# Startup of a fused strided-sparse attention and ELU MLP kernel: fills ahead of loads, 80-row loads, and a new order of work

## The chip, the core and the metric

The kernel runs on one core of a Trainium2 chip. The metric is the device time of one execution in microseconds (us). The core has TensorE (PE; its weight loads are listed as PEld), VectorE (DVE), ScalarE (ACT), GpSimd (POOL) and SyncE (SP). Each takes its own instructions in program order and waits for the others by semaphores. Data moves by DMA, issued from SP, ACT or POOL.

## The reference

```python
# q, k, v: (8 batches, 8 heads, 576 positions, 64) fp32
scores = q @ k.T / 8                       # per batch and head
rel = pos[:, None] - pos[None, :]
mask_local   = (rel >= 0) & (rel < 32)                     # heads 0 to 3
mask_strided = (rel >= 0) & (pos_q % 32 == pos_k % 32)     # heads 4 to 7
attn = softmax(where(mask, scores, -1e9))
x = (attn @ v), heads side by side         # 4608 tokens x 512
h = x @ w_in                               # 512 -> 2048
out = elu(h) @ w_out                       # 2048 -> 512, fp32
```

## The kernel before

**Layout.** A position is written as p*8 + s, with s from 0 to 7 and p from 0 to 71. A load "by runs" (`load_runs`) brings, for each of four heads, 72 rows p of 8*64 elements, each row one run of 2 KB of fp32 in DRAM, and the POOL queue casts it to bf16 on the way. Strided attention (`s`) then only needs keys and queries with the same s modulo 4; local attention (`l`) works in windows of 96 queries and 128 keys. The tiles of a batch are called qs, ks, vs, ql, kl (by runs) and vl (six blocks of 96 rows for each head, in `vl_t`). Batch 1 is loaded into borrowed space: the end of `xT` and of `g[1]`.

**Attention.** Four pairs of heads for each batch: `0s0`, `0s1`, `0l0`, `0l1` for batch 0 and so on. For each pair q and k are transposed (batches 0 to 2 on PE, token `T`, copied out of PSUM by `c` on DVE or `C` on ACT; later ones by DMA, tokens `X` and `P`). For each half u of a pair: scores `S` (PE), exp `e` (ACT), mask `m` (DVE), product with v and row sums `O` (PE), log `n` and exp `r` of the sums (ACT, a reciprocal), and `x` (DVE), which writes the 512-wide activations `xT`.

**MLP.** Nine chunks of 512 tokens. For each of the 16 blocks of 128 hidden units: `L` (or its halves `a` and `b`) is the first product, `h` exp on ACT, `i` (DVE) or `j` (ACT) the clamp, `g` (DVE) the ELU into `g[0]` or `g[1]`. `Z.chunk.k.part` is the second product, `o` or `q` the copy out of PSUM (ACT or DVE), `t` the store. PSUM has eight banks; the last number of a token is the bank.

**Order.** Everything is written out by hand in the string `ORDER`: one token after another, and each engine takes its instructions in the order of the tokens. `D.x.b` is a load issued on POOL (`D.wi0` to `D.wi3` are the quarters of w_in, `D.wo0` to `D.wo3` those of w_out), `V` and `W` copies of v on DVE. `w` is a run of 42 matmuls on zeros at the start, and `K` casts the first pair's q (DVE) and k (ACT), which arrive as fp32 in `stage`, a piece of `g[0]`. `F` tokens are fills on DVE: `F.v0`, `F.v1` and `F.vs` write the constant columns of `vl_t[0]`, `vl_t[1]` and `vs_p`; `F.ks0` and the like write zeros into the half of the padded k tiles `kp` that no head uses; `F.ms` and `F.ml` make the masks, the latter from `mask_1`, which POOL makes.

**Before the tokens** there is a short prologue: the two stage loads (q on SP, k on ACT), the loads of qs and ks for heads 2 and 3 of the strided group, three memsets on DVE, then on POOL the loads of vs, ql, kl, vl, and after them `iota` and `mask_1`. In the tokens that follow, `F.v0` (L347) stands on DVE behind the load into the same tile `vl_t[0]` (L253), ahead of `F.ms`, both `K.q` and everything later on DVE:

```python
w.7.42 F.ks0 F.ks1 F.kl0 F.v1 F.vs F.v0 F.kl1 F.ms K.q.1 F.ml D.wi0.0 K.q.0 K.k.0 D.wi1.0 T.0s0.q.0
K.k.1 c.0s0.q T.0s0.k.7 D.wi2.0 T.0s1.q.6 c.0s0.k c.0s1.q D.wi3.0 S.0s0.1.01 S.0s0.0.23 e.0s0.1
```

**The end.** `copy_o` has a special case for the token `8.3` (`LAST`): the copy is cut in two halves, one on ACT and one on DVE, and its second store goes on ACT's queue. The order before ends with `Z.8.3`, `o.8.3`, `t.8.3`.

Of the kernel before, what the change touches and what calls it, by code (L numbers as in the profile page):

```python
# [15 lines left out]
S = 576  # L16
# [19 lines left out]
w.7.42 F.ks0 F.ks1 F.kl0 F.v1 F.vs F.v0 F.kl1 F.ms K.q.1 F.ml D.wi0.0 K.q.0 K.k.0 D.wi1.0 T.0s0.q.0  # L36
K.k.1 c.0s0.q T.0s0.k.7 D.wi2.0 T.0s1.q.6 c.0s0.k c.0s1.q D.wi3.0 S.0s0.1.01 S.0s0.0.23 e.0s0.1
T.0s1.k.7 e.0s0.0 m.0s0.1 c.0s1.k m.0s0.0 S.0s1.1.67 S.0s1.0.01 D.qs.1 e.0s1.1 O.0s0.1.23 e.0s1.0
D.ks.1 m.0s1.1 O.0s0.0.67 n.0s0.1 m.0s1.0 T.0l0.q.0 r.0s0.1 n.0s0.0 x.0s0.1 O.0s1.1.45 r.0s0.0
c.0l0.q D.vs.1 T.0l0.k.3 x.0s0.0 n.0s1.1 r.0s1.1 T.0l1.q.6 c.0l0.k T.0l1.k.7 x.0s1.1 C.0l1.q D.ql.1  # L40
V.0 S.0l0.1.01 S.0l0.0.56 c.0l1.k e.0l0.1 O.0s1.0.34 e.0l0.0 m.0l0.1 S.0l1.0.01 n.0s1.0 m.0l0.0
O.0l0.1.56 e.0l1.0 D.kl.1 r.0s1.0 m.0l1.0 S.0l1.1.01 n.0l0.1 x.0s1.0 e.0l1.1 O.0l0.0.34 r.0l0.1
m.0l1.1 O.0l1.0.01 x.0l0.1 n.0l0.0 O.0l1.1.56 r.0l0.0 D.vl.1 n.0l1.0 x.0l0.0 a.0.1.7 r.0l1.0 n.0l1.1
x.0l1.0 a.0.0.4 r.0l1.1 a.0.3.0 x.0l1.1 b.0.1 D.wo0.0 b.0.0 h.0.1 b.0.3 h.0.0 i.0.1 a.0.7.5 h.0.3
g.0.1 a.0.4.6 j.0.0 b.0.4 i.0.3 a.0.8.7 g.0.3 D.wo1.0 h.0.4 a.0.12.3 i.0.4 b.0.12 g.0.0 a.0.13.0
h.0.12 b.0.13 D.wo2.0 g.0.4 a.0.14.4 h.0.13 i.0.12 b.0.14 g.0.12 j.0.13 T.1s1.q.6 a.0.6.1 D.wo3.0
c.1s1.q h.0.14 b.0.8 g.0.13 a.0.9.6 h.0.8 i.0.14 b.0.7 D.fqs.0 g.0.14 j.0.8 a.0.2.0 b.0.9 h.0.7
g.0.8 a.0.5.4 h.0.9 i.0.7 a.0.10.3 D.fks.0 i.0.9 b.0.6 g.0.7 a.0.15.7 h.0.6 b.0.2 g.0.9 D.fql.0
b.0.15 h.0.2 i.0.6 b.0.10 g.0.6 h.0.15 b.0.5 h.0.10 i.0.2 T.1s0.k.6 T.1s0.q.5 i.0.15 D.qs.2 h.0.5
T.1l0.q.1 i.0.10 C.1s0.q a.0.11.2 g.0.15 b.0.11 C.1l0.q g.0.2 T.1s1.k.7 h.0.11 T.1l0.k.5 g.0.10  # L50
T.1l1.k.0 C.1s0.k i.0.5 T.1l1.q.1 D.ks.2 C.1l0.k i.0.11 Z.0.1.0.3 c.1l1.k C.1l1.q C.1s1.k g.0.11
S.1l1.1.56 S.1s0.0.01 e.1l1.1 g.0.5 Z.0.3.0.7 e.1s0.0 m.1l1.1 V.1 D.ql.2 S.1s1.0.45 S.1s1.1.01
e.1s1.0 Z.0.1.1.3 m.1s0.0 e.1s1.1 m.1s1.0 O.1l1.1.45 m.1s1.1 O.1s1.0.01 n.1l1.1 Z.0.3.1.7 r.1l1.1
n.1s1.0 D.kl.2 x.1l1.1 Z.0.1.2.3 r.1s1.0 x.1s1.0 O.1s1.1.45 Z.0.3.2.7 n.1s1.1 r.1s1.1 O.1s0.0.01
x.1s1.1 D.vs.2 Z.0.1.3.3 n.1s0.0 r.1s0.0 D.vl.2 S.1l0.1.45 o.0.1 x.1s0.0 Z.0.3.3.7 e.1l0.1 t.0.1
S.1l1.0.01 m.1l0.1 o.0.3 S.1s0.1.23 S.1l0.0.45 Z.0.0.0.6 e.1l1.0 t.0.3 e.1l0.0 m.1l1.0 O.1l0.1.01
Z.0.0.1.6 e.1s0.1 m.1l0.0 n.1l0.1 m.1s0.1 O.1l0.0.23 r.1l0.1 O.1s0.1.45 x.1l0.1 n.1l0.0 Z.0.0.2.6
n.1s0.1 r.1l0.0 r.1s0.1 Z.0.0.3.6 x.1l0.0 x.1s0.1 O.1l1.0.01 o.0.0 T.2s1.k.2 W.2 Z.0.2.0.3 n.1l1.0
t.0.0 r.1l1.0 c.2s1.k Z.0.2.1.3 x.1l1.0 V.2 L.1.2.0 L.1.1.1 h.1.2 i.1.2 L.1.0.2 h.1.1 g.1.2 L.1.8.4
i.1.1 h.1.0 g.1.1 j.1.0 L.1.5.0 h.1.8 g.1.0 L.1.4.1 h.1.5 i.1.8 i.1.5 L.1.6.2 h.1.4 g.1.8 Z.0.2.2.3  # L60
i.1.4 h.1.6 g.1.5 j.1.6 Z.0.2.3.3 g.1.4 g.1.6 T.2s1.q.0 o.0.2 L.1.7.1 c.2s1.q t.0.2 S.2s1.0.23 h.1.7
T.2s0.k.0 T.2s0.q.4 e.2s1.0 i.1.7 T.2l1.q.5 D.qs.3 c.2s0.q C.2s0.k L.1.3.6 g.1.7 C.2l1.q D.ks.3
m.2s1.0 S.2s0.0.34 h.1.3 T.2l1.k.5 D.vs.3 e.2s0.0 O.2s1.0.01 i.1.3 L.1.9.7 c.2l1.k n.2s1.0 m.2s0.0
L.1.11.2 r.2s1.0 g.1.3 h.1.9 O.2s0.0.34 x.2s1.0 h.1.11 T.2l0.q.6 T.2l0.k.5 n.2s0.0 i.1.9 D.ql.3
c.2l0.q L.1.15.0 r.2s0.0 g.1.9 L.1.10.1 i.1.11 h.1.15 x.2s0.0 C.2l0.k S.2s0.1.67 g.1.11 S.2s1.1.34
h.1.10 L.1.14.5 X.ks.3 i.1.15 e.2s0.1 i.1.10 D.kl.3 e.2s1.1 L.1.13.2 g.1.15 h.1.14 g.1.10 S.2l1.1.34
h.1.13 L.1.12.0 i.1.14 X.qs.3 m.2s0.1 j.1.13 g.1.14 O.2s0.1.67 e.2l1.1 Z.1.0.0.1 g.1.13 n.2s0.1
D.vl.3 m.2l1.1 P.s.3 h.1.12 S.2l0.0.23 S.2l1.0.45 m.2s1.1 Z.1.0.1.1 r.2s0.1 i.1.12 e.2l1.0 g.1.12
Z.1.0.2.1 e.2l0.0 x.2s0.1 O.2s1.1.45 m.2l0.0 O.2l1.1.23 n.2s1.1 S.2l0.1.67 W.3 Z.1.0.3.1 n.2l1.1
X.kl.3 m.2l1.0 r.2s1.1 Z.1.1.0.0 o.1.0 x.2s1.1 Z.1.1.1.0 r.2l1.1 D.qs.4 X.ql.3 e.2l0.1 x.2l1.1  # L70
O.2l0.0.45 D.ks.4 Z.1.1.2.0 n.2l0.0 m.2l0.1 D.vs.4 O.2l0.1.67 r.2l0.0 S.3s1.0.23 t.1.0 Z.1.2.0.1
n.2l0.1 x.2l0.0 e.3s1.0 Z.1.1.3.0 r.2l0.1 m.3s1.0 O.3s1.0.23 x.2l0.1 o.1.1 S.3s1.1.45 Z.1.2.1.1
n.3s1.0 t.1.1 e.3s1.1 O.2l1.0.67 Z.1.3.0.0 r.3s1.0 m.3s1.1 P.l.3 n.2l1.0 x.3s1.0 O.3s1.1.45
Z.1.3.1.0 X.ks.4 r.2l1.0 n.3s1.1 S.3s0.0.23 x.2l1.0 Z.1.3.2.0 e.3s0.0 r.3s1.1 L.2.8.6 m.3s0.0
x.3s1.1 L.2.4.7 h.2.8 D.ql.4 i.2.8 O.3s0.0.45 h.2.4 L.2.10.2 g.2.8 n.3s0.0 i.2.4 L.2.2.3 h.2.10
g.2.4 r.3s0.0 L.2.9.6 i.2.10 h.2.2 g.2.10 L.2.5.7 D.kl.4 h.2.9 i.2.2 x.3s0.0 j.2.9 L.2.1.2 g.2.2
h.2.5 S.3l1.0.45 g.2.9 h.2.1 L.2.11.3 e.3l1.0 i.2.5 i.2.1 L.2.6.6 h.2.11 D.vl.4 g.2.5 X.kl.4
S.3l0.1.45 g.2.1 h.2.6 L.2.7.7 i.2.11 e.3l0.1 i.2.6 L.2.14.2 m.3l1.0 h.2.7 m.3l0.1 O.3l1.0.45 g.2.6
h.2.14 Z.1.3.3.0 g.2.11 n.3l1.0 L.2.15.6 i.2.7 r.3l1.0 i.2.14 g.2.7 o.1.3 L.2.0.3 h.2.15 x.3l1.0
t.1.3 L.2.3.7 h.2.0 i.2.15 g.2.14 O.3l0.1.45 h.2.3 L.2.13.0 g.2.15 n.3l0.1 i.2.3 L.2.12.2 i.2.0  # L80
r.3l0.1 g.2.3 h.2.13 Z.1.2.2.1 x.3l0.1 h.2.12 S.3l1.1.67 i.2.13 S.3l0.0.45 e.3l1.1 g.2.0 Z.1.2.3.1
X.ql.4 e.3l0.0 g.2.13 S.3s0.1.67 o.1.2 Z.2.1.0.3 m.3l1.1 m.3l0.0 e.3s0.1 i.2.12 O.3l1.1.01 Z.2.2.0.4
X.qs.4 m.3s0.1 n.3l1.1 g.2.12 O.3s0.1.67 r.3l1.1 Z.2.2.1.4 W.4 n.3s0.1 x.3l1.1 P.l.4 Z.2.2.2.4
r.3s0.1 x.3s0.1 Z.2.2.3.4 P.s.4 O.3l0.0.67 o.2.2 Z.2.1.1.3 t.1.2 n.3l0.0 Z.2.1.2.3 r.3l0.0 t.2.2
Z.2.0.0.4 x.3l0.0 L.3.4.7 D.qs.5 L.3.5.6 D.ks.5 h.3.4 i.3.4 L.3.3.5 D.vs.5 h.3.5 g.3.4 D.ql.5
L.3.9.0 i.3.5 h.3.3 g.3.5 j.3.3 S.4s1.0.12 L.3.11.7 h.3.9 g.3.3 e.4s1.0 L.3.0.6 i.3.9 h.3.11 m.4s1.0
S.4s0.0.12 g.3.9 h.3.0 X.ks.5 L.3.10.5 i.3.11 e.4s0.0 i.3.0 L.3.8.0 h.3.10 m.4s0.0 g.3.0 j.3.10
D.kl.5 O.4s1.0.12 Z.2.0.1.4 g.3.11 n.4s1.0 g.3.10 h.3.8 O.4s0.0.67 Z.2.0.2.4 r.4s1.0 i.3.8 n.4s0.0
g.3.8 L.3.6.5 x.4s1.0 r.4s0.0 D.vl.5 Z.2.0.3.4 h.3.6 x.4s0.0 L.3.2.2 i.3.6 o.2.0 g.3.6 S.4s1.1.01
t.2.0 h.3.2 L.3.13.4 e.4s1.1 i.3.2 X.kl.5 L.3.12.5 g.3.2 h.3.13 m.4s1.1 j.3.13 L.3.1.0 h.3.12 g.3.13  # L90
O.4s1.1.12 h.3.1 S.4l0.1.67 i.3.12 Z.2.3.0.4 n.4s1.1 g.3.12 e.4l0.1 Z.2.1.3.3 i.3.1 r.4s1.1 m.4l0.1
S.4l0.0.67 g.3.1 o.2.1 L.3.7.5 x.4s1.1 e.4l0.0 t.2.1 L.3.14.3 h.3.7 m.4l0.0 i.3.7 O.4l0.1.67 h.3.14
O.4l0.0.12 g.3.7 L.3.15.0 n.4l0.0 i.3.14 n.4l0.1 Z.2.3.1.4 g.3.14 r.4l0.0 Z.2.3.2.4 r.4l0.1 x.4l0.0
h.3.15 Z.2.3.3.4 x.4l0.1 i.3.15 S.4l1.0.12 o.2.3 Z.3.1.0.7 g.3.15 e.4l1.0 t.2.3 Z.3.1.1.7 m.4l1.0
O.4l1.0.01 S.4s0.1.23 n.4l1.0 S.4l1.1.45 Z.3.1.2.7 X.qs.5 e.4s0.1 r.4l1.0 Z.3.1.3.7 m.4s0.1 e.4l1.1
x.4l1.0 O.4s0.1.23 o.3.1 Z.3.0.0.6 P.s.5 m.4l1.1 n.4s0.1 W.5 O.4l1.1.01 X.ql.5 r.4s0.1 Z.3.0.1.6
n.4l1.1 D.qs.6 x.4s0.1 Z.3.0.2.6 r.4l1.1 D.ks.6 Z.3.3.0.7 P.l.5 x.4l1.1 D.vs.6 Z.3.0.3.6 t.3.1
S.5s1.1.01 o.3.0 S.5s1.0.23 S.5s0.0.45 e.5s1.0 L.4.3.6 t.3.0 e.5s1.1 m.5s1.0 L.4.2.3 e.5s0.0 m.5s1.1
D.ql.6 h.4.3 X.ks.6 O.5s1.1.01 m.5s0.0 O.5s1.0.45 h.4.2 i.4.3 L.4.7.2 n.5s1.0 g.4.3 Z.3.3.1.7
n.5s1.1 i.4.2 r.5s1.0 g.4.2 L.4.0.6 r.5s1.1 x.5s1.0 D.kl.6 h.4.7 L.4.9.3 x.5s1.1 h.4.0 O.5s0.0.45  # L100
i.4.7 h.4.9 S.5l1.0.01 i.4.0 Z.3.3.2.7 n.5s0.0 g.4.7 e.5l1.0 g.4.0 L.4.1.2 r.5s0.0 i.4.9 D.vl.6
m.5l1.0 S.5s0.1.01 h.4.1 L.4.13.6 x.5s0.0 P.s.6 e.5s0.1 i.4.1 O.5l1.0.45 g.4.9 h.4.13 S.5l0.1.01
X.qs.6 Z.3.3.3.7 n.5l1.0 m.5s0.1 i.4.13 e.5l0.1 L.4.8.3 g.4.1 r.5l1.0 g.4.13 O.5s0.1.12 o.3.3 X.kl.6
L.4.15.0 x.5l1.0 h.4.8 n.5s0.1 L.4.11.7 W.6 h.4.15 i.4.8 D.qs.7 S.5l0.0.45 m.5l0.1 r.5s0.1 t.3.3
Z.4.0.0.6 g.4.8 D.ks.7 h.4.11 x.5s0.1 L.4.4.3 e.5l0.0 D.vs.7 i.4.15 j.4.11 O.5l0.1.45 m.5l0.0 h.4.4
L.4.10.1 g.4.15 n.5l0.1 i.4.4 L.4.6.0 g.4.11 h.4.10 r.5l0.1 i.4.10 L.4.12.2 g.4.4 h.4.6 L.4.14.7
# [47 lines left out]
def kernel(  # L154
# [150 lines left out]
    for nm in ("vs", "ql", "kl", "vl"):  # L305
        load(nm, 0)
# [406 lines left out]
```

## Time and profile before

| | before |
|---|---|
| median of 3 runs | 334.99 us (334.53 to 335.02) |
| the profiled execution's own time | 334.41 us |
| its span | 332.7 us, so 1.7 us lie around the span |
| PE busy | 307.3 us (92%) |
| DVE, ACT busy | 228.0 us (69%), 234.4 us (70%) |
| mean granted TensorE clock | 0.997 |
| DMA | 38.61 MB in 99319 packets; POOL's queue (q0) 18.66 MB, SP's (q1) 19.10 MB, ACT's (q10) 0.44 MB |

The profile gives one execution. Times count from the start of the span. In the timeline a row is start, duration, engine, line, operation, tiles and count; in brackets stands how long the engine was idle before it and what ended that. A busy PE is modelled and is not PE at its peak. DMA bytes are counted at the destination, so a casting load from fp32 counts half of what it reads.

### The profile page before, as it was taken

The page shows a single profiled execution, that of the slowest core. Times are in us where ns is not written, and L with a number is a line of the kernel's source. Part 1 is how long each engine was busy: PE and PEld are TensorE (multiplying, and loading weights), DVE is VectorE, ACT ScalarE, POOL GpSimd, SP SyncE. Part 2 cuts the span into 40 slices and gives each one's busy share as a digit, 9 for nine tenths or more (in the row PEclk, how much of TensorE's full clock was granted, in tenths as well). Part 3 has the DMA queues.
Part 4 walks back from the last instruction along what each step waited for, and adds up shares of the span by engine and source line. Part 5 has one row for each costly group of instructions (what it writes and reads, how often), then busy time and mean ns, then how long its engine had stood idle before and what let it go on. Part 6 is the DMA issues. An engine that isn't in the chain of part 4 may idle for free.

```text
span 332.7 us, 6428 instructions
## 1 busy us (share of the span) xinstructions
PE 307.3 (92%) x2410; PEld 158.8 (48%) x2410; DVE 228.0 (69%) x452; ACT 234.4 (70%) x408; POOL 75.6 (23%) x102
## 2 busy tenths in 40 slices
PE   5069999999989999999999999999999999999993
PEld 5056454446445445455554454455544444444441
DVE  5168796578966996788579979874589386447500
ACT  2038687868988897799799889689798675336320
POOL 8634230003920722630263205400000000000000
PEclk9999999999999999999999999999999999999998
DMA  7999997215999999999799989962400121111032
GB/s 148 187 206 188 206 196 69 65 32 92 155 183 140 184 134 180 169 94 141 155 208 129 175 152 157 110 163 61 131 14 0 35 62 32 33 34 53 10 92 69
DMA packets 99319, 38.61 MB, mean 116 GB/s; under 512 B 80568, under 2 KB 93112, under 8 KB 99288
## 3 DMA queue, kind: packets, MB, share of 16 engines
q0 software_dynamic: 65920, 18.66, 56.7%
q1 hardware_dynamic: 33128, 19.10, 27.1%
q10 hardware_dynamic: 240, 0.44, 0.4%
q8 instruction: 19, 0.31, 0.4%
q14 instruction: 12, 0.10, 0.1%
HBM read 37.84 MB, written 9.44 MB: 142 GB/s over the span
## 4 chain that ended last, share of the span: by engine, by line
PE 63%; DVE 12%; DMA 9%; ACT 8%; issue 4%; POOL 1%; SPq 0%; ACTq 0%; POOLq 0%; DVEq 0%
PE ps L636 30%; PE ps L602 25%; DVE g L630 4%; PE ps L440 3%; DVE he L619 3%; DMA kpl<-kTl 3%; DMA vl<-in_v_dram 3%; ACT e L447 3%; DVE xT L569 2%; DMA kTs<-ks 2%; ACT ln L538 2%; ACT he L610 2%; DMA kps<-kTs 2%; PE ps L510 1%; ACT rc L544 1%
## 5 line engine op out<-in xcount | busy, mean ns | idle before, releaser
L636 PE MATMUL ps<-w_out_sb,g 128*128 128x512 bf16 x576 | 136.6, 379 | 0.0
L602 PE MATMUL ps<-xT,w_in_sb 128*128 128x512 bf16 x576 | 135.1, 381 | 1.0 <-DVE g L630 0.8
L610 ACT ACTIVATE he<-ps 128x512 f32<-128x512 f32 x144 | 83.5, 595 | 31.8 <-PE ps L602 30.7
L602 PEld LDWEIGHTS <-w_in_sb 128*128 128x128 bf16 x576 | 54.5, 98 | 63.8 <-issue 4.7
L630 DVE TENSOR_TENSOR g<-he,ps 128x512 bf16<-128x512 bf16 x118 | 78.4, 681 | 6.4 <-PE ps L636 4.1
L636 PEld LDWEIGHTS <-g 128*128 128x128 bf16 x576 | 52.7, 98 | 56.3 <-DVE g L630 0.6
L619 DVE TENSOR_SCALAR he<-he 128x512 bf16<-128x512 f32 x118 | 50.9, 442 | 23.1 <-ACT he L610 22.4
L569 DVE TENSOR_TENSOR xT<-ps,rc 64x576 bf16<-64x576 f32 (+1 forms) x64 | 43.2, 679 | 23.2 <-ACT rc L544 22.3
L447 ACT ACTIVATE e<-ps 72x576 bf16<-72x576 f32 (+1 forms) x64 | 40.3, 647 | 18.0 <-PE ps L440 17.0
L538 ACT ACTIVATE ln<-ps 64x576 f32<-64x576 f32 (+1 forms) x64 | 36.9, 583 | 8.7 <-PE ps L510 6.2
L544 ACT ACTIVATE rc<-ln 64x576 f32<-64x576 f32 (+1 forms) x64 | 39.4, 620 | 1.5
L650 ACT COPY osb<-ps 128x512 f32<-128x512 f32 x32 | 18.7, 585 | 24.4 <-PE ps L636 24.3
L236 POOL DMA_DIRECT2D ql<-in_q_dram x20 | 16.5, 832 | 30.7 <-DMA qTl<-ql 27.9
L454 DVE TENSOR_TENSOR pm<-e,mask_s 72x576 bf16<-72x576 bf16 x32 | 14.4, 452 | 13.2 <-ACT e L447 12.8
L229 POOL DMA_DIRECT2D qs<-in_q_dram x7 | 5.5, 787 | 77.7 <-DMA qTs<-qs 45.3
L628 DVE SCALAR_TENSOR_TENSOR g<-he,ps 128x512 bf16<-128x512 bf16 x26 | 17.7, 680 | 1.1 <-ACT he L617 0.8
L460 DVE TENSOR_TENSOR pm<-e,mask_l 128x576 bf16<-128x576 bf16 x32 | 14.3, 453 | 4.5 <-ACT e L447 3.9
L617 ACT ACTIVATE he<-he 128x512 bf16<-128x512 f32 x26 | 16.4, 629 | 0.7
L243 POOL DMA_DIRECT2D kl<-in_k_dram x20 | 15.2, 776 | 5.8 <-DMA vs<-in_v_dram 2.8
L400 PE MATMUL ps<-identity,qs 72*128 72x72 bf16 x32 | 2.2, 226 | 12.8 <-DVE qs L387 12.8
L510 PEld LDWEIGHTS <-vl 128*128 128x128 bf16 x144 | 8.7, 96 | 6.4 <-issue 1.9
L503 PEld LDWEIGHTS <-vsp 72*128 72x128 bf16 x192 | 9.1, 98 | 5.4 <-issue 0.7
(91 smaller groups left out, 185.9 us busy)
## 6 DMA issues: line engine op xcount, KB each, us to landing
out_dram<-osb SPq DMA_DIRECT2D x31, 144.0 KB
vl<-in_v_dram POOLq DMA_DIRECT2D x8, 288.0 KB, 8.0
w_in_sb<-in_moe_w_in_dram POOLq DMA_DIRECT2D x4, 512.0 KB, 12.4
w_out_sb<-in_moe_w_out_dram POOLq DMA_DIRECT2D x4, 512.0 KB, 14.9
vs<-in_v_dram POOLq DMA_DIRECT2D x7, 288.0 KB, 7.5
qs<-in_q_dram POOLq DMA_DIRECT2D x6, 288.0 KB, 6.5
ks<-in_k_dram POOLq DMA_DIRECT2D x6, 288.0 KB, 8.6
kps<-kTs SPq DMA_DIRECT2D x10, 160.0 KB
```

The source lines that it names most:

```text
L236: nc.gpsimd.dma_start(out=t[0:RS, h % 2, :, h // 2, :], in_=q[b, h].rearrange("(p s) d -> p s d", s=NS))
L447: nc.scalar.activation(e[0:R], tiles.pop(("S", key, u))[0:R], ACT.Exp, scale=scale)
L538: nc.scalar.activation(t, s_ps, ACT.Ln)
L544: nc.scalar.activation(t, tiles.pop(("ln", key, u)), ACT.Exp, scale=-1.0)
L569: nc.vector.tensor_mul(dst, o_ps, rc)
L602: nc.tensor.matmul(tiles["h", ch, m], lhsT=w_in_sb[:, c, m * 128:(m + 1) * 128], rhs=xT[:, c, ch * CHUNK:(ch + 1) * CHUNK], start=(c == 2) ...
L610: nc.scalar.activation(e, tiles["h", i[0], i[1]], ACT.Exp)
L619: eng.tensor_scalar(e1, e, scalar1=1.0, scalar2=1.0, op0=ALU.min, op1=ALU.subtract)
L628: nc.vector.scalar_tensor_tensor(dst, e1, -1.0, h, op0=ALU.mult, op1=ALU.max)
L630: nc.vector.tensor_tensor(dst, e1, h, op=ALU.max)
L636: nc.tensor.matmul(ops, lhsT=g[ch % 2][:, m, kk * 128:(kk + 1) * 128], rhs=w_out_sb[:, m, :], start=(m == 0), stop=(m == MC - 1), skip_gro ...
L650: eng(o_sb, o_ps)
```

## The change

- **Fills first.** The fills of both `vl_t` tiles stand in the prologue on DVE, ahead of the loads into them; that of `vs_p` follows. The `F` tokens for them are gone, and so are those for `kp`.
- **Zeros on ScalarE.** The four zero halves of `kp` (64 x 664 or 64 x 592 32-bit words) are written by four ACT copies of a broadcast zero, right after ACT's table load; only the small edges stay on DVE.
- **iota** goes ahead of the loads on POOL.
- **80 rows.** `load_runs` and the stage loads bring 80 rows of a head instead of 72; rows 72 to 79 belong to the next head and fill what the DMA transposes read beyond the data. Where that would run past the tensor's end, 72 are kept. The three small loads that filled those rows before (`fill_rows`, tokens `D.fqs`, `D.fks`, `D.fql`) are gone.
- **One queue.** Both stage loads are issued on SP, q first.
- **F.ml** makes the mask by two copies with a broadcast instead of six.
- **A new order.** All tokens from the first to the last are arranged anew. Counts are the same but for: `c` 14 to 18 and `C` 10 to 6, `o` 33 to 32 and `q` 3 to 4. The order now ends with `Z.8.0.3 o.8.0 t.8.0`; token `8.3` is the last but one.

```diff
-    raw["vs"] = consts.tile([RS, HG * NS * D], BF16, tag="vs", name="vs")
+    raw["vs"] = consts.tile([RP, HG * NS * D], BF16, tag="vs", name="vs")
...
+    def runs(x, b, h, n):
+        rows = RP if (b * H + h + n - 1) * S + RP * NS <= B * H * S else RS
+        return rows, bass.AP(x.tensor, x.offset + (b * H + h) * S * D,
+                             [[NS * D, rows], [S * D, n], [1, NS * D]])
     def load_runs(nm, b, h0=0, n=HG):
...
-            out=t[0:RS].rearrange("p (h f) -> p h f", h=HG)[:, h0:h0 + n],
-            in_=x[b, hb:hb + n].rearrange("h (p s) d -> p h (s d)", s=NS))
+            out=rawof(nm, b)[0:rows].rearrange("p (h f) -> p h f", h=HG)[:, h0:h0 + n], in_=in_)
...
-    load_stage(nc.sync, 0, q)
-    load_stage(nc.scalar, 1, k)
+    load_stage(0, q)
+    load_stage(1, k)
...
+    nc.gpsimd.iota(dist, pattern=[[1, RS]], base=RS, channel_multiplier=-1)
+    for t in vl_t:
+        fill_ones(t, HG * LB)
+        nc.vector.memset(blocks(t, HG * LB)[0:PRE, 0, :], 0.0)
     for nm in ("vs", "ql", "kl", "vl"):
         load(nm, 0)
-    nc.gpsimd.iota(dist, pattern=[[1, RS]], base=RS, channel_multiplier=-1)
+    fill_ones(vs_p, HG * NS)
...
+    for (c, z), t in kp.items():
+        s_ = slice(2 * NS * RP, None) if c == "s" else slice(0, PRE)
+        nc.vector.memset(t[z * D:(z + 1) * D, s_], 0.0)
+        r = slice((1 - z) * D, (2 - z) * D)
+        w = t[r].bitcast(F32)
+        nc.scalar.copy(w, zero[r, 0:2].bitcast(F32).to_broadcast([D, w.shape[1]]))
...
             for u in range(2):
-                for i in range(3):
-                    nc.vector.tensor_copy(mask_l[:, u, :, i, :], mask_1)
+                nc.vector.tensor_copy(mask_l[:, u],
+                                      mask_1.unsqueeze(2).to_broadcast([128, NS, 3, LN]))
...
 ORDER
-w.7.42 F.ks0 F.ks1 F.kl0 F.v1 F.vs F.v0 F.kl1 F.ms K.q.1 F.ml D.wi0.0 K.q.0 K.k.0 D.wi1.0 T.0s0.q.0
-K.k.1 c.0s0.q T.0s0.k.7 D.wi2.0 T.0s1.q.6 c.0s0.k c.0s1.q D.wi3.0 S.0s0.1.01 S.0s0.0.23 e.0s0.1
+w.7.42 F.ms K.q.1 K.q.0 D.wi0.0 F.ml T.0s0.q.0 D.wi1.0 c.0s0.q K.k.0 K.k.1 D.wi2.0 T.0s1.q.0
+T.0s0.k.1 c.0s1.q D.wi3.0 T.0s1.k.2 c.0s0.k c.0s1.k S.0s0.0.01 S.0s0.1.67 e.0s0.0 S.0s1.1.45
...
-Z.8.2.3.1 Z.7.2.3.2 o.8.2 Z.8.1.0.1 t.8.2 o.7.2 Z.8.0.0.0 t.7.2 Z.8.0.1.0 Z.8.0.2.0 Z.8.0.3.0
-Z.8.1.1.1 o.8.0 Z.8.1.2.1 t.8.0 Z.8.1.3.1 Z.8.3.0.0 o.8.1 Z.8.3.1.0 t.8.1 Z.8.3.2.0 Z.8.3.3.0 o.8.3
-t.8.3
+t.7.1 o.7.2 L.8.5.1 t.7.2 h.8.0 i.8.0 L.8.7.7 h.8.5 g.8.0 L.8.2.6 i.8.5 h.8.7 g.8.5 L.8.3.0 h.8.2
+i.8.7 g.8.7 L.8.14.1 h.8.3 i.8.2 L.8.9.7 i.8.3 h.8.14 g.8.2 L.8.10.2 g.8.3 h.8.9 i.8.14 Z.8.2.0.0
+i.8.9 h.8.10 g.8.14 j.8.10 Z.8.2.1.0 g.8.9 g.8.10 Z.8.1.0.1 Z.8.2.2.0 Z.8.2.3.0 Z.8.1.1.1 o.8.2
+Z.8.1.2.1 t.8.2 Z.8.1.3.1 Z.8.3.0.0 o.8.1 Z.8.3.1.0 t.8.1 Z.8.3.2.0 Z.8.3.3.0 Z.8.0.0.1 o.8.3
+Z.8.0.1.1 t.8.3 Z.8.0.2.1 Z.8.0.3.1 o.8.0 t.8.0
```

## The prediction

> **What bounds the kernel now.** I read the page's slices first, then the list of waits, then the timeline of the first 50 us, and last the timeline of the end.
>
> ```profile
> PE   5069999999989999999999999999999999999993
> ...
> DMA  7999997215999999999799989962400121111032
> GB/s 148 187 206 188 206 196 69 65 32 92 155 183 140 184 134 180 169 94 141 155 208 129 175 152 157 110 163 61 131 14 0 35 62 32 33 34 53 10 92 69
> ```
>
> One slice is 8.3 us. From the fourth on PE is busy nine tenths; its hole is the second slice. DMA is full for six slices, to about 50 us.
>
> ```profile
> PE ps L400 <- DVE qs L387: 12.8, 1, 12.8
> ...
> DVE vl L347 <- DMA vl<-in_v_dram: 9.0, 1, 9.0
> ```
>
> PE waits once, 12.8 us, for DVE's cast of q, and DVE waited 9.0 us for a load before that. In order of time:
>
> ```profile
> 5.45 1.20 POOL L253 DMA_DIRECT2D vl<-in_v_dram  x1
> ...
> 6.36 1.14 ACT L387 CAST ks<-g 72x512 bf16<-72x512 f32 x2 [3.61 <-DMA g<-in_k_dram]
> ...
> 14.89 0.70 DVE L347 MEMSET vl<- 128x768 f32 x1 [8.95 <-DMA vl<-in_v_dram]
> ...
> 17.00 0.42 DVE L387 CAST qs<-g 72x512 bf16<-72x512 f32 x1
> ...
> 18.56 0.66 PE L400 MATMUL ps<-identity,qs 72*128 72x72 bf16 x8 [12.84 <-DVE qs L387]
> ...
> 20.72 1.19 ACT L447 ACTIVATE e<-ps 72x576 bf16<-72x576 f32 x2 [13.22 <-PE ps L440]
> ```
>
> The fill of vl waits for the load of the same tile, which lands near 14.8. k was cast at 6.36, and q's load was issued at the same time as k's: the first transposes wait for a fill that they don't need. The first exp starts at 20.72, the last `x` of batch 0 ends at 33.98 (33.52 + 0.46), and from 32.1 PE has the MLP to work on.
>
> **Part 1: the wait goes, and what is late next.** (a) DVE. The fills start after `mask_1`, at 1.22. From before's rows: each vl tile 0.70 + 0.09 + 0.07, twice 1.72; vs_p 0.91 + 0.09; ones, kTs, kTl 0.34; four small edges 0.08 + 0.08 + 0.07 + 0.07. That ends at 4.6. `F.ms` is 0.19 + 0.20 + 0.23 with gaps: 5.3. Its iota is ready at 3.6, since POOL does it after `identity` (3.36). The load of vl on POOL now waits for the fill, done at 2.1, and is issued only near 5.6: no cost. (b) q. No row shows its landing; k's row bounds it: not after 6.4 if q lands like k, and not before DVE is free at 5.3. I take 6.0, as q is first on its queue: casts 0.42 + 0.54, 7.0. (c) `F.ml` stands on DVE between the casts and `c.0s0.q`, and needs `mask_1` from POOL, which was done at 7.51 (7.20 + 0.31) and stays there, since iota has only changed places. So 7.55, and the six copies took 0.84 for the same elements that two now write, plus 0.10: 8.5. This is the next late thing. (d) `c.0s0.q` 0.46 (9.0), `T.0s1.q` 0.66 into the same bank (9.65), `c.0s1.q`, `c.0s0.k` 0.46 each (10.6), and from the end of the k copy (20.20) to the first exp (20.72) there were 0.52: first exp at 11.1, against 20.72, **9.6 us earlier**.
>
> Beside it lies k: ACT's table load ends at 2.75, then four zero copies. No row shows them; between 0.585 (128x512, L650) and 0.8 each, near the 0.65 of a 576-wide exp: 2.6 us, done at 5.4 (6.0 at most). k is issued 0.42 later (SP's issue of q takes 0.42), so 6.36 + 0.42 = 6.8, casts to 7.95: hidden under (c). Cover gone, it would cost nothing before 9.7, when `T.0s0.k` is due.
>
> (e) Batch 0's attention took 13.26 us from the first exp to the last `x`, with ACT nearly full: 8 exps of 0.65, 8 logs of 0.40, 8 exps of 0.44 and a copy of 0.64 are 12.6. The copy moves to DVE (`c.0l1.q`, 0.46), where it and `V.0` (0.55) now stand ahead of the mask `m.0l0.1` that PE and ACT wait for. I take no change, with -0.6 (the copy) and +1.0 (those two) as ends. The last `x` ends at 24.4. Sum of part 1: **-9.6** (-10.2 to -8.6).
>
> **Part 2: do the loads follow?** POOL's loads share eight semaphores, so each waits until the load eight before it has landed, and POOL's own waits tell the landings.
>
> ```profile
> 31.29 0.58 POOL L259 DMA_DIRECT2D qs<-in_q_dram  x1 [1.53 <-DMA g<-in_v_dram]
> ...
> 35.32 0.92 POOL L229 DMA_DIRECT2D qs<-in_q_dram  x1 [1.96 <-PE ps L602]
> ```
>
> Here the first wait is for vs of batch 1, and the last, though put down to PE, is for vl. Counted so through the timeline, w_in's quarters landed at 17.5, 20.2, 22.5 and 25.1, batch 1's q and k (strided) at 27.1 and 29.0, vs 31.3, ql 31.9, kl 32.8, vl 35.3, and w_out's at 37.8, 40.3, 42.8, 46.1. The queue runs at about 200 GB/s throughout, so an earlier PE brings nothing earlier. 80 rows add 32 KB to each load of 288 KB: for the nine such loads' worth of batches 0 and 1, 288 KB, 1.4 us. The three fill loads that go (96 KB, 0.5 us) came later. So batch 1 and w_out land up to 1.4 later.
>
> When are they due? After 24.4 PE does `a` and `b` halves at 2 x 0.216 (28 L602 matmuls took 6.04) and transposes at about 0.35. `T.1s1.q` comes after nine halves, 28.3, against 28.0 to 28.5; `T.1s0.k` near 30.1, against 30.4; `T.1l1.k` near 34, against 34.2. `V.1` stands on DVE behind 11 `g` (0.69), 9 `i` (0.43) and two copies (0.46): 12.4, with the first `h` near 25.4 about 37.4, against 36.7. `Z.0.0.0` comes at about 40, against 39.2, and its four parts follow at w_out's pace of 2.5 us. Everything is due within half a microsecond of its landing. I take **+1.0**, between 0 and 4 (if PE waits for each of w_out's parts, its last at 47.5 would stand against some 44 to 46).
>
> The rows again by the skill: 240 packets on q10 are 216 runs of data (144 for k, 72 for the last store) and 24 more, 12 for each of its two transfers. The Trainium skill, "DMA: Bandwidth & Descriptors", section "Why a DMA increments its semaphore by 16 and not by 1", says that a copy is spread over the largest number up to 16 that divides its slowest dimension, which makes 12 engines of 72 rows and 16 of 80. By that rule the stage loads alone would be some 0.2 us quicker, an estimate; the rows show a queue bounded by bytes, so the sum has nothing for it.
>
> A row also speaks on the clock: 8 transposes took 0.66 at 18.56 and 0.42 at 39.93, both at granted clock 1.00. The Trainium skill, "TensorE: Matmul & The Clock Gate", section "What's actually happening", has the array at half rate after about 3.4 us idle; by it the idle stretch before, 12.8 us, ends cold, while a gap of 2 us after the 42 zero matmuls need not. By an estimate from that rule the start would win up to 0.5 us more. The sum uses the slow row.
>
> **Part 3: the middle.** The work on PE from the first `L.1` on is the same, and PE's idle time between 32 and 300 us is 5.0 us by its windows (0.42, 1.58, 0.88, 0.69, 0.75, 0.67, 0). Four PSUM copies move from ACT to DVE (about 2 us of DVE, at 69%), `i` and `j` keep their counts. A new order can win back those 5.0 or add as much; nothing in the trace tells which, and I take **0**, between -3 and +3.
>
> **Part 4: the end.**
>
> ```profile
> 327.72 0.37 ACT L647 COPY osb<-ps 128x256 f32<-128x256 f32 x1 [2.87 <-PE ps L636]
> 328.12 0.42 DVE L648 COPY osb<-ps 128x256 f32<-128x256 f32 x1 [15.53 <-ACT osb L647]
> 328.57 0.32 SPq L663 DMA_DIRECT2D out_dram<-osb  x1
> 328.58 0.35 ACTq L663 DMA_DIRECT2D out_dram<-osb  x1
> ```
>
> Before this the last 80 matmuls run without a gap, 17.43 us from 310.21 to 327.64, and the last stores are issued 0.94 after PE's end, on two queues at once. In the new order eight `L.8` stand together and then `Z.8.2`. On DVE they cost seven `i` and eight `g`, 8.5 us from the first `h`, against 7 x 0.86 = 6.0 for PE: `Z.8.2.0` waits for `g.8.3` about 0.4, `Z.8.2.2` for `g.8.10` about 0.4. The last block is now 8.0: its tokens cross a row of the output twice, so one whole copy (0.59) and three stores on SP (0.36 each): the last is issued 0.08 + 0.59 + 0.05 + 0.72 = 1.44 after PE's end, 0.5 later. **+1.3**, between 0.3 and 2.
>
> **Sum.** -9.6 + 1.0 + 0 + 1.3 = -7.3. The profiled execution took 334.41 (332.7 + 1.7), so 327.1; the median of the runs lies 0.58 above it: **327.7 us**. About 0.2% (0.7 us) is what this kernel's runs can tell from no change.
>
> **Rivals.** *The queue is the bound* (0.17): the start is won and given back while PE waits for batch 1 and w_out. For: landings and needs coincide in part 2. Against: before's order left `V.1` at 52.18, 17 us after its landing, and the new one needs only 9.6 of that. At its end, +4 instead of +1, and +2 in the middle: 332.7; as a case 330 to 333. *Better than the sum* (0.15): the new order also loses less in the middle (-3) and the queue costs nothing (-1): 323.7. *Slower* (0.05): 80-row loads run slower than the 72-row ones. DVE would stand at `V.1`, with the copies `c.1s0.q`, `c.1s1.k`, the next `i` and `g` queued behind it, and PE behind those. It decides when vl of batch 1 lands 7.3 us later than 36.7, at 44, that is if the queue falls from about 200 GB/s to about 165; at 150 it lands at 49, and the time is 340. Nothing in the rows asks for that: the slices with 72-row and 128-row loads have the same rate. *DVE is held all the same* (0.01): another load, say the stage's, holds the casts until the vl landing, and the time is that of before, 335.0.
>
> **Chances.** Forecast 0.62 (325.5 to 330), queue 0.17, better 0.15, slower 0.05, no change 0.01. Faster: 0.62 + 0.17 + 0.15 = 0.94. The range takes the forecast's ends and most of both neighbours: 323.4 to 332.2.
>
> **What would show it.** Right: no wait of DVE for a load of vl, the first exp near 11, the last `x` of batch 0 near 24.4, `V.1` near 37, eight L602 groups with a short PE gap near the end. Wrong: `c.0s0.q` much after 9; POOL's slot waits ending more than 2 us later than the landings above; PE idle over 5 us between 25 and 50; PE's idle time from 60 on far from 5 us.

## The result, and the profile after

| | before | after |
|---|---|---|
| median (runs) | 334.76 us (4) | 325.92 us (4: 324.66 to 327.68) |
| ratio, 95% interval | | 0.9746 [0.9708, 0.9783] |
| the profiled execution: time, span | 334.41, 332.7 us | 326.53, 324.7 us |
| PE busy | 307.3 us | 308.3 us |
| first exp starts | 20.72 us | 9.86 us |
| last `x` of batch 0 ends | 33.98 us | 22.91 us |
| last matmul ends | 327.64 us | 319.70 us |

The kernel is 8.8 us faster by the medians; 327.7 had been forecast. Ratios here use each kernel's fast runs alone; the only run that counts as slow, over 1.5% above the fastest of its kernel, is one of experiment 5. The slices of the page, 8.1 us each:

```profile
PE   6899999999997999999999989999999999999993
...
PEclk9559999999997999999999999999999999999999
DMA  8999999799999866997499969742501101112122
GB/s 172 194 206 197 204 206 137 120 184 124 198 165 172 173 116 163 180 150 142 115 189 121 115 168 92 100 115 81 126 2 32 47 19 33 32 29 56 46 67 66
```

The hole of PE in the second slice has gone, and DMA is full for six or seven slices, as before. The granted clock is 0.5 in slices two and three, and drops once more in the thirteenth. The first of these is not a loss against before: the trace of before holds no record of the clock earlier than 33.96 us, and the page fills that stretch with 1.00. Sixteen transposes of ql took the same time in both kernels, before (first line) and after, where the clock is recorded at 0.50 (last line: a window of 2 us with the busy time of PE, PEld, DVE, ACT and POOL, then the clock, the DMA share and GB/s):

```profile
24.02 0.69 PE L403 MATMUL ps<-identity,ql 72*64 72x72 bf16 x16
```

```profile
12.31 0.69 PE L401 MATMUL ps<-identity,ql 72*64 72x72 bf16 x16
```

```profile
10.00:12.00 2.00, 1.49 (x37) 1.42 (x33) 1.15 (x3) 1.96 (x4) 1.40 (x3) 0.50 1.87 177
```

The list of waits (who waited for whom: total in us, times, longest) has no row of DVE for a load of vl any more. PE's longest wait, 12.8 us before, is now 1.6 us, for a copy by DMA in the middle of the kernel:

```profile
PE ps L438 <- DMA kpl<-kTl: 1.6, 1, 1.6
...
PE ps L398 <- DVE qs L385: 1.4, 1, 1.4
...
PE ps L438 <- DMA qTl<-ql: 1.3, 1, 1.3
```

The timeline of the start (start, duration, engine, line; in brackets the idle time before and what ended it):

```profile
1.36 0.70 DVE L307 MEMSET vl<- 128x768 f32 x1
...
2.10 1.50 ACT L334 COPY kps<-zero 64x664 f32<-64x664 f32 x2
...
5.13 1.18 POOL L256 DMA_DIRECT2D vl<-in_v_dram  x1
...
5.56 1.14 ACT L385 CAST ks<-g 72x512 bf16<-72x512 f32 x2 [0.58 <-DMA g<-in_k_dram]
5.58 1.43 DVE L385 CAST qs<-g 72x512 bf16<-72x512 f32 x2
...
7.07 0.43 PE L398 MATMUL ps<-identity,qs 72*128 72x72 bf16 x8 [1.35 <-DVE qs L385]
...
7.21 0.38 DVE L345 COPY mask_l<-mask 128x288 bf16<-128x288 bf16 x2 [0.20 <-POOL mask L321]
...
9.86 2.41 ACT L445 ACTIVATE e<-ps 72x576 bf16<-72x576 f32 x4 [3.16 <-PE ps L438]
```

The fill of vl stands at 1.36 and waits for nothing; it stood at 14.89. ACT's idle time before the first exp was 13.22 us and is 3.16. The end:

```profile
305.72 13.98 PE L634 MATMUL ps<-w_out_sb,g 128*128 128x512 bf16 x64
...
319.73 0.58 ACT L648 COPY osb<-ps 128x512 f32<-128x512 f32 x1 [3.04 <-PE ps L634]
```

Before the last block PE doesn't stop: the 64 matmuls run from 305.72 to 319.70 in one piece.

### The profile page after: what moved, and what is told of

Read it like the earlier page. It is cut to its first block, busy times and chain, and to the rows that moved or that the text cites. A ratio compares the mean times of both kernels' runs of the same rounds, so it can differ in the third digit from the quotient of the medians.

```text
span 324.7 us, 6422 instructions
## 1 busy us (share of the span) xinstructions
PE 308.3 (95%) x2410; PEld 158.8 (49%) x2410; DVE 227.3 (70%) x449; ACT 234.3 (72%) x407; POOL 72.3 (22%) x99
## 4 chain that ended last, share of the span: by engine, by line
PE 58%; DVE 14%; ACT 11%; DMA 8%; issue 5%; POOL 2%; SPq 1%; POOLq 0%; DVEq 0%; ACTq 0%
PE ps L634 28%; PE ps L600 22%; DVE g L628 5%; ACT ln L536 4%; PE ps L438 4%; DVE xT L567 4%; DVE he L617 3%; ACT rc L542 3%; DMA qTs<-qs 3%; DMA kpl<-kTl 2%; ACT e L445 2%; DMA ks<-in_k_dram 2%; PE ps L508 1%; DMA qTl<-ql 1%; ACT he L608 1%
## 5 line engine op out<-in xcount | busy, mean ns | idle before, releaser
L634 PE MATMUL ps<-w_out_sb,g 128*128 128x512 bf16 x576 | 137.5, 382 | 0.4 <-DVE g L628 0.3
L634 PEld LDWEIGHTS <-g 128*128 128x128 bf16 x576 | 53.3, 98 | 57.6 <-issue 1.3
L617 DVE TENSOR_SCALAR he<-he 128x512 bf16<-128x512 f32 x118 | 52.1, 455 | 22.2 <-ACT he L608 21.6
L536 ACT ACTIVATE ln<-ps 64x576 f32<-64x576 f32 (+1 forms) x64 | 36.9, 582 | 5.6 <-PE ps L508 2.5
L458 DVE TENSOR_TENSOR pm<-e,mask_l 128x576 bf16<-128x576 bf16 x32 | 14.4, 451 | 11.1 <-ACT e L445 11.0
L233 POOL DMA_DIRECT2D qs<-in_q_dram x7 | 4.8, 688 | 42.9 <-DMA qTs<-qs 24.4
L438 PE MATMUL ps<-qTl,kpl 128*128 128x96 bf16 x120 | 8.6, 208 | 2.9 <-DMA kpl<-kTl 1.6
```

The source lines that it names most:

```text
L438: nc.tensor.matmul(dst, lhsT=kt[pr, k0:k0 + 128], rhs=rhs, start=True, stop=True, skip_group_check=True)
L536: nc.scalar.activation(t, s_ps, ACT.Ln)
L617: eng.tensor_scalar(e1, e, scalar1=1.0, scalar2=1.0, op0=ALU.min, op1=ALU.subtract)
L634: nc.tensor.matmul(ops, lhsT=g[ch % 2][:, m, kk * 128:(kk + 1) * 128], rhs=w_out_sb[:, m, :], start=(m == 0), stop=(m == MC - 1), skip_gro ...
```

## The experiments

Every ratio is against the kernel before, run on the same chip (334.83 us in the first four experiments, 334.36 us in the others). "Start" is the first exp. "Rest" is the time from the end of batch 0's last `x` to the last matmul's end, in the profiled execution: 293.7 us before, 296.8 after.

**1. The fills alone.** The kernel before, with the fills of vl ahead of the loads, that of vs_p right behind them, and nothing else changed.

```diff
-w.7.42 F.ks0 F.ks1 F.kl0 F.v1 F.vs F.v0 F.kl1 F.ms K.q.1 F.ml ...
+w.7.42 F.ks0 F.ks1 F.kl0 F.kl1 F.ms K.q.1 F.ml ...
...
+    for t in vl_t:
+        fill_ones(t, HG * LB)
+        nc.vector.memset(blocks(t, HG * LB)[0:PRE, 0, :], 0.0)
     for nm in ("vs", "ql", "kl", "vl"):
         load(nm, 0)
+    fill_ones(vs_p, HG * NS)
```

> The kernel before with one part alone: the fills of vl and vs_p stand ahead of the loads; order, 72 rows, two stage queues and zeros on VectorE stay. If the wait behind the load is the whole cause, VectorE's chain is: fills to 4.0, four zero fills 2.75, masks 0.7, casts and mask copies 1.9, and the first exp comes near 12 (20.72 before, 9.86 in the changed kernel): 326 to 327.5 us. If the new order or the 80 rows brought most of it, the old order, laid out for a start at 32 us, gives the lead back in waits of TensorE: 331 us or more.

Measured: 325.82 us, ratio 0.9742 [0.9695, 0.9788]. Start 12.18, rest 293.4.

```profile
12.18 1.18 ACT L457 ACTIVATE e<-ps 72x576 bf16<-72x576 f32 x2 [4.77 <-PE ps L450]
```

Moving these fills brings as much time as the whole change. The start is 8.5 us earlier than before, the last matmul's end 8.8 us. So the other edits and the new order, together, are worth nothing that the times show, though they start the exps 2.3 us earlier still.

**2. The fill back behind the load.** The changed kernel with the fill of `vl_t[0]` after the load into it.

```diff
-        fill_ones(t, HG * LB)
...
+    fill_ones(vl_t[1], HG * LB)
     for nm in ("vs", "ql", "kl", "vl"):
         load(nm, 0)
     fill_ones(vs_p, HG * NS)
+    fill_ones(vl_t[0], HG * LB)
```

> The changed kernel with one part undone: the fill of the first vl tile stands behind the load into it. If the wait is the cause, VectorE sits idle from about 4 to 14, the first exp comes near 19.5 to 20, and the time is that of before or a little more, 333 to 337. If the rest of the change carries the gain, 326 to 329.

Measured: 336.95 us (10 runs), ratio 1.0079 [1.0043, 1.0115]. Start 19.98, rest 296.3. The wait is back:

```profile
13.91 0.70 DVE L307 MEMSET vl<- 128x768 f32 x1 [10.52 <-DMA vl<-in_v_dram]
...
19.98 2.41 ACT L446 ACTIVATE e<-ps 72x576 bf16<-72x576 f32 x4 [13.14 <-PE ps L439]
```

With this one wait put back, the rest of the change leaves the kernel 0.8% slower than before. The two experiments together show that the wait is the cause of the gain.

**3. The old order.** The changed kernel with the order of before (without the `F` tokens and the small loads that are gone).

```diff
-w.7.42 F.ms K.q.1 K.q.0 D.wi0.0 F.ml T.0s0.q.0 ...
+w.7.42 F.ms K.q.1 F.ml D.wi0.0 K.q.0 K.k.0 D.wi1.0 T.0s0.q.0 ...
```

> The changed kernel with the order of before (its fill tokens taken out). If the prologue brings the gain and the middle of the new order loses 3 us against the old one, as the two traces show (lead 11.3 us after batch 0, 7.9 at the end), the first exp is near 10 and the time 323 to 325, below the changed kernel. If the old order needs its late start, because batch 1 and w_out land no earlier, it loses the lead between 25 and 60 us: 329 or more.

Measured: 323.79 us, ratio 0.9688 [0.9638, 0.9739]. Start 9.93, rest 293.2; the last matmul ends at 316.35, against 319.70 with the new order. The old order starts as early, keeps the whole shift of 11 us, and its rest is 3.6 us shorter in these two profiles; by the medians it is 2.1 us faster, with intervals that overlap. It loses 2.3 us of its own in one wait (`PE ps L438 <- DMA kps<-kTs`), of which the last experiment makes use.

**4. 72 rows.** The changed kernel, with 72 rows a head in the loads of batches 0 and 1 and of the stage.

```diff
-        rows = RP if (b * H + h + n - 1) * S + RP * NS <= B * H * S else RS
+        rows = RP if b > 1 and (b * H + h + n - 1) * S + RP * NS <= B * H * S else RS
```

> The changed kernel with 72 rows in all loads of batches 0 and 1, the stage loads too (80 from batch 2 on). The prediction charged the added rows 1.4 us of queue time. If bytes bound the queue, everything lands up to 1.4 earlier and the time is 325 to 326, not above the changed kernel. If 80 rows spread better over the engines, the first cast of k moves from 5.56 to 6.3, vl of batch 1 lands no earlier, and the time is the same or up to 1 us above.

Measured: 327.82 us, ratio 0.9802 [0.9759, 0.9845]; start 10.71, rest 296.8. The same slot wait on POOL, which tells when the first quarter of w_out had landed, first with 72 rows, then, in the changed kernel, with 80:

```profile
39.15 0.64 POOL L233 DMA_DIRECT2D vs<-in_v_dram  x1 [1.39 <-DMA w_out_sb<-in_moe_w_out_dram]
```

```profile
37.33 0.64 POOL L233 DMA_DIRECT2D vs<-in_v_dram  x1 [1.61 <-DMA w_out_sb<-in_moe_w_out_dram]
```

With a tenth less data it comes 1.8 us later in this pair; at most 0.55 of that can be a later issue ahead of it, since w_in's quarters are issued from 7.68 instead of 7.13. Counted through the timeline, batch 1's q and k land at 28.7 and 29.9 (80 rows: 26.5 and 28.1), its vl at 36.9 (35.1).

One pair of executions doesn't give the size of this. By the same waits, w_out's first quarter lands at 37.8 (before), 38.5 (experiment 1) and 39.2 us in the three kernels with 72 rows, and between 37.2 and 38.3 in the seven with 80; experiments 1 and 3, which share the old order, differ by 0.2. For batch 1's vs the two groups are apart, but only just: 31.1 to 33.0 and 29.9 to 31.0. So 80 rows land no later, against the forecast; how much earlier isn't shown.

The time follows the start: 0.85 us later there, 0.81 at the last matmul. The landings themselves cost PE nothing that this shows. And 0.55 of the 0.85 come by a chain that the forecast named: the 72-row loads occupy POOL 0.70 to 0.84 us each, those of 80 rows 0.61 to 0.77, so `mask_1` is ready later, and the copies of `F.ml` start at 7.76 (here after 1.55 us of idle time) instead of 7.21. The other 0.3 is PE's: its second eight transposes took 0.64 us instead of 0.42 and the next sixteen 1.15 instead of 0.69, since the clock, by the trace's records, fell to 0.5 at 7.4 us and not at 9.3.

**5. P.l.3 ahead of X.ks.4.** In the changed kernel the copies of token `P.l.3` on SP stand behind the transposition `X.ks.4`, which waits for its load until 90.4 us.

```diff
-... g.1.9 X.ks.4 h.2.1 ... g.2.1 e.3s0.0 P.l.3 i.1.15 ...
+... g.1.9 P.l.3 X.ks.4 h.2.1 ... g.2.1 e.3s0.0 i.1.15 ...
```

> The changed kernel with one token moved: P.l.3, the two copies into the padded k tiles, stands on SyncE ahead of X.ks.4 instead of behind it. In the changed kernel's trace X.ks.4 waits on SyncE for a load until 90.4, the copies start at 92.1 and land at 100.5, TensorE idles 1.6 us for them, and then its granted clock is 0.5 for 3.4 us. If that place is where the new order loses its 3 us, the copies start near 84, land before 93, the clock stays at 1.00, and the time falls by 2 to 3.5 us, to 322.5 to 324. If the loss lies elsewhere or only moves, 325 to 326.

Measured: 323.45 us (323.38, 323.45 and 325.77); ratio 0.9687 [0.9643, 0.973], an interval that overlaps the changed kernel's. Start 9.74, rest 293.8. The place in the changed kernel:

```profile
90.44 1.56 SPq L587 DMA_TRANSPOSE kTs<-ks  x1
...
92.09 1.24 SPq L593 DMA_DIRECT2D kpl<-kTl  x2
...
100.58 0.39 PE L438 MATMUL ps<-qTl,kpl 128*128 128x96 bf16 x5 [1.64 <-DMA kpl<-kTl]
...
101.06 3.22 PE L634 MATMUL ps<-w_out_sb,g 128*128 128x512 bf16 x8
```

and with the token moved:

```profile
83.49 1.19 SPq L593 DMA_DIRECT2D kpl<-kTl  x2
...
90.80 0.40 PE L438 MATMUL ps<-qTs,kps 128*128 128x72 bf16 x7 [1.65 <-DMA kps<-kTs]
91.43 1.48 SPq L587 DMA_TRANSPOSE kTs<-ks  x1
```

The copies are issued 8.6 us earlier and PE's wait for kpl is gone. So is what followed it: eight L634 matmuls took 3.22 us, against 1.89 elsewhere, since the clock was down for 3.41 us (the windows of the changed kernel show 0.50 from 102 to 104, those of this one 1.00). But another wait has come, 1.65 us for kps. To weigh the one against the other, number PE's weight loads in order of time (each of these runs records 2410), take the same one in each run, and see how many us later (+) or earlier (-) it starts than in this run:

| weight load (its time here) | after | 72 rows | two queues | zeros on DVE | fill behind |
|---|---|---|---|---|---|
| 880 (77.1) | +0.42 | +1.53 | +0.87 | +1.83 | +10.35 |
| 940 (90.9) | -0.95 | -0.07 | -0.11 | +1.00 | +8.82 |
| 1180 (122.2) | +1.20 | +1.83 | +1.96 | +3.99 | +12.64 |
| 1600 (180.3) | +1.52 | +2.50 | +2.00 | +3.98 | +12.96 |
| 1840 (214.4) | +3.14 | +3.95 | +3.87 | +5.62 | +12.80 |
| last (316.0) | +3.13 | +3.95 | +3.87 | +5.62 | +12.80 |

Where the order differs, between 77 and 122 us, the moved token is worth 0.3 to 2.3 us net. Another 1.6 to 2.1 us lie between 122 and 214, where the orders are the same, and "fill behind" doesn't lose them either. So this edit is only part of what it seemed to bring. Nor does the loss need the step of the clock: the runs of 72 rows and two queues have none between 25 and 320 us, and their rest is 296.8 and 297.1. What goes with the second loss is a wait on SP, here in SP's own list of waits, for the changed kernel and for this one:

```profile
SPq L593 <- DMA kTl<-kl: 2.9, 1, 2.9
```

```profile
SPq L593 <- DMA kTl<-kl: 1.1, 1, 1.1
```

It is 2.9 to 3.7 us in the four kernels that lose there, 1.1 and 0.3 in the two that don't. The copies to kpl wait in SP's queue for a DMA transposition, the transposition `X.ql.6` stands behind them (issued at 189.10), and PE waits 1.29 us for that. That this wait causes the second loss is argued, not shown, and why the transposition lands late in some executions stays open.

**6. Two queues.** The changed kernel with the stage's k loaded on ACT's queue, as before.

```diff
-    load_stage(0, q)
-    load_stage(1, k)
+    load_stage(nc.sync, 0, q)
+    load_stage(nc.scalar, 1, k)
```

> The changed kernel with k's stage load issued on ScalarE again, beside q's on SyncE, both with 80 rows. If the order on one queue is what lets q and k land by 5.6, k comes no later here (issued 0.47 us earlier) but q later, and ScalarE's table load and zero copies start 0.67 later, hidden: first exp at 9.9 within 0.3, the time within 0.7 us of the changed kernel. If one queue was a real gain, the first exp is near 10.5 or later.

Measured: 326.79 us, ratio 0.9747 [0.9707, 0.9787]; start 10.31, rest 297.1. k's casts start at 5.97 and q's at 5.72, against 5.56 and 5.58. This later landing is hidden: in both kernels the first transposes start at 7.07 and the copies of `F.ml` at 7.21. The 0.45 us of the start arise behind that, on PE. The same sixteen transposes of k, here and in the changed kernel:

```profile
8.62 1.16 PE L398 MATMUL ps<-identity,ks 72*128 72x72 bf16 x16
```

```profile
8.31 0.69 PE L398 MATMUL ps<-identity,ks 72*128 72x72 bf16 x16
```

By the trace's records the clock fell to 0.5 at 7.2 us here and at 9.3 in the changed kernel. So one queue neither gains nor costs anything that shows.

**7. Zeros on DVE.** The changed kernel with the zero halves of kp as memsets on DVE.

```diff
-        w = t[r].bitcast(F32)
-        nc.scalar.copy(w, zero[r, 0:2].bitcast(F32).to_broadcast([D, w.shape[1]]))
+        nc.vector.memset(t[r], 0.0)
```

> The changed kernel with the four zero halves written on VectorE, in the prologue, instead of ScalarE: four memsets of 0.55 to 0.61, 2.3 us, ahead of the masks. The masks were done at 5.66 and q's casts waited for nothing more, so the casts end 2.3 later, at 9.3, the mask copies no longer wait for GpSimd, and the first exp comes at 11.8 to 12.1: the time rises by 2 us to 328. If VectorE still had slack there, it stays at 326.

Measured: 329.85 us, ratio 0.9853 [0.9813, 0.9892]; start 12.48, rest 296.7.

```profile
8.16 0.92 DVE L384 CAST qs<-g 72x512 bf16<-72x512 f32 x2
...
12.48 0.65 ACT L444 ACTIVATE e<-ps 72x576 bf16<-72x576 f32 x1 [5.60 <-PE ps L437]
```

The casts of q start 2.6 us later and end 2.1 later (9.08 against 7.01). The exp starts 2.6 later, as the first transposes took 0.66, 0.64 and 1.16 us against 0.43, 0.42 and 0.69; 2.5 us of it arrive at the last matmul. The zeros on ACT are the second working part of the change.

**8. The old order, tuned.** Experiment 3 with two edits of its order: `F.ml` goes behind `c.0s1.q`, since nothing needs it sooner and it waits for `mask_1`; and batch 3's first scores, which wait for kps, come some tokens later, behind two parts of `Z`.

```diff
-w.7.42 F.ms K.q.1 F.ml D.wi0.0 K.q.0 ... c.0s0.k c.0s1.q D.wi3.0
+w.7.42 F.ms K.q.1 D.wi0.0 K.q.0 ... c.0s0.k c.0s1.q F.ml D.wi3.0
...
-r.2l0.0 S.3s1.0.23 t.1.0 Z.1.2.0.1 n.2l0.1 x.2l0.0 e.3s1.0 Z.1.1.3.0 r.2l0.1 m.3s1.0 O.3s1.0.23
-x.2l0.1 o.1.1 S.3s1.1.45 Z.1.2.1.1 n.3s1.0
+r.2l0.0 t.1.0 Z.1.2.0.1 n.2l0.1 x.2l0.0 Z.1.1.3.0 S.3s1.0.23 r.2l0.1 e.3s1.0 x.2l0.1 o.1.1
+m.3s1.0 S.3s1.1.45 Z.1.2.1.1 O.3s1.0.23 n.3s1.0
```

> The changed kernel's prologue with the order of before, and two edits to that order: F.ml goes behind c.0s1.q, so that q's casts and copies do not wait for the mask from GpSimd, and S.3s1.0 with its exp stands two Z blocks later, where the copies into the padded k tile have landed. Old order with this prologue ran in 323.8. F.ml: first exp from 9.93 to 8.9 to 9.2. S.3s1.0: TensorE's wait of 2.5 us for those copies falls below 1. Sum 321 to 322.5. If these waits were cover for others, 323.5 to 324.5.

Measured: 322.15 us (6 runs), ratio 0.9631 [0.9598, 0.9665], the fastest here: its interval lies below that of the changed kernel, though it overlaps that of experiment 3. Start 9.09, rest 292.1. PE's wait for kps is gone from the list; by the same weight loads as above it is 0.8 to 1.1 us ahead of experiment 3 up to the wait, 2.5 to 3.6 just behind it, and 1.9 at the end.

```profile
9.09 1.18 ACT L445 ACTIVATE e<-ps 72x576 bf16<-72x576 f32 x2 [2.33 <-PE ps L438]
```

## Why the prediction was right, by its own steps

The sum was -7.3 us. The last matmul ends 7.94 us earlier, and the profiled execution took 7.88 us less (326.53 against 334.41). All four terms were off: three by 1.0 to 1.5 us too late, one by 3.1 us too early. The cause was right; that the sum came within 0.7 us is luck, since these errors nearly cancel.

**Part 1, the start: right mechanism, sized too small.** Forecast -9.6, measured -11.1 at the last `x` (-10.9 at the first exp; the attention between took 13.05 us, against 13.26). (a) and (b) hold: the fills end at 4.81, the casts of q at 7.01 (forecast 4.6 and 7.0). (c) was the step that missed: `mask_1` was ready at 7.18, not 7.51, and the two copies of `F.ml` took 0.38 instead of 0.84, so `c.0s0.q` starts at 7.56 and not at 8.5. That `F.ml` and its wait for POOL come next was right: experiment 4 delays `mask_1` and with it the start, and experiment 8, which moves `F.ml` away, starts 0.84 us before experiment 3, though the clock fell at 7.3 us there and at 9.0 in experiment 3. (d) missed by the clock: the transposes took 0.43 and 0.42 for eight, not 0.66. k was cast at 5.56, not 6.8, and the four zero copies took 0.69 to 0.75 each (2.9 together, forecast 2.6); both stay hidden, as forecast. Some of the start is luck of the execution too: in the changed kernel the clock fell only at 9.3 us, behind these transposes; where it fell at 7.2 (experiment 6), the same chain gave -10.4.

The forecast set the two rates of the transposes, 0.66 and 0.42, beside "granted clock 1.00". At 18.56 that 1.00 was no reading, since the record of before begins only at 33.96 us. The records of experiment 4 begin sooner, and there eight transposes take 0.43 us at 6.27 and 0.64 us at 8.57, in these windows (columns as in the section on the result):

```profile
6.00:7.00 1.00, 0.43 (x8) 0.34 (x9) 0.21 (x1) 0.93 (x2) 1.00 (x1) 1.00 1.10 151
...
8.00:9.00 1.00, 0.43 (x8) 0.42 (x8) 0.52 (x3) 0.00 (x0) 1.00 (x2) 0.50 1.20 178
```

So 0.66 is, within 0.02, the time at half clock. The forecast took it for its sum and set "up to 0.5 us more" outside; the one transposition of the chain was 0.24 us shorter.

**Part 2, the queue: wrong sign.** Forecast +1.0 for 80 rows, by bytes. Landings in the changed kernel are up to 1.3 us earlier (batch 1's q 26.5 against 27.1, vs 30.0 against 31.3, vl 35.1 against 35.3, w_out's first quarter 37.3 against 37.8; only kl, 33.3 against 32.8, is later). Experiment 4 and the landings listed there speak against the count by bytes: 11% more bytes came no later. Why, the runs don't show. The rule of the Trainium skill, "DMA: Bandwidth & Descriptors", section "Why a DMA increments its semaphore by 16 and not by 1", which the forecast weighed and left out of its sum (72 rows go to 12 engines, 80 to 16), has the right sign. The same section has an exception: on this chip some direct copies on a software queue, as POOL's is, get all 16 engines and the rows are shared out over them. The views don't say which engines a load used, so that the rule is the mechanism isn't shown. The landings had a margin in any case: PE's idle time from 32 to 60 us is 0.45 us. The needs weren't as forecast either: `V.1` ran at 36.0, not 37.4 (the forecast's own terms, 25.4 + 12.4, give 37.8), and its "within half a microsecond" passed over gaps of 0.7 and 0.8 in its own list, at `V.1` and `Z.0.0.0`. So the term is 0, and the rival "the queue is the bound" falls.

**Part 3, the middle: forecast 0, between -3 and +3; measured +3.1,** just past that end. It is the new order's: with the old one (experiments 1 and 3) the rest is 293.2 to 293.4 us, with the new one 296.3 to 297.1 in five kernels of six. In the profile, PE's idle time between 32 and 300 us went from 5.0 to 6.7 us, and 3.41 us at half clock cost up to 1.7 more (two kernels lose as much without that step, as experiment 5 says). By the aligned loads of experiment 5 two places stand out, SP's queue around 90 us and around 187 us, where copies to kpl and a transposition stand behind one that waits. For the first, the moved token shows 0.3 to 2.3 us; the second is argued. The forecast gave no term to SP's tokens `X` and `P`, which the new order also moves past one another; that was the step left out.

**Part 4, the end: forecast +1.3, measured 0.** The stall before `Z.8.2`, 0.8 us, didn't come: PE runs its last 64 matmuls without a gap, and from the last matmul to the end of the span it takes 5.0 us, as before (5.06). The three stores of the last block cost nothing that the span shows.

**The rivals.** "Better than the sum" had a queue that costs nothing, which was so, and 3 us less in the middle, which was not. "Slower" was to come from slow 80-row loads; they landed no later. "DVE is held all the same" is the case of experiment 2: with a fill behind its load the change measures 1.0079.

## What to carry to other kernels

A tile that is partly filled and partly loaded is filled first, before the load is issued: one memset behind a load held a whole engine's queue for 9 us, and moving it was worth all that this rewrite was worth. When many edits are made at once, each is to be run alone: here the good ones hid a new order that gave about 3 us back in five profiles of six, and the old order with two small edits is the fastest kernel. When an order is weighed, the queue of DMA issues counts as an engine: a copy behind a transposition that waits for its load comes as late as that load.

## What the runs showed of the hardware

- **More rows, no later landing.** 80 rows of 2 KB in place of 72, 11% more bytes, landed batch 1's vs at 29.9 to 31.0 us in seven kernels, against 31.1 to 33.0 in three, and POOL spent 0.61 to 0.77 us on an issue instead of 0.70 to 0.84 (experiment 4).
- **The clock falls in steps of 3.41 us.** By the trace's records it is at 0.5 in the changed kernel from 9.3 to 23.0 us, four times 3.41, though PE was busy with attention's short matmuls for 1.49 to 2.00 of every 2 us, and for one step from 101.5 us after a gap of 1.64 us. Gaps of 1.65 us (experiment 5) and 2.30 us (experiment 3) drew no such step. The Trainium skill, "TensorE: Matmul & The Clock Gate", section "What's actually happening", has a window of 3.41 us that runs freely, and that agrees with the length of the steps and with gaps that only sometimes count.
- **Transposes show the clock.** Eight transposes took 0.43 us where the clock is recorded at 1.00 and 0.64 to 0.66 us where it is at 0.50 (experiments 4 and 2). The first fall came at 7.2 to 9.7 us in the seven executions of the changed prologue whose record begins before it; a fall at 7.4 and 7.2 instead of 9.3 goes with a start 0.3 and 0.45 us later in experiments 4 and 6.
